# Top-k attention and a SwiGLU FFN on one core: when the first units' attention ends, and when FFN pieces may run

## Chip, core and metric

The kernel runs on one core of one Trainium2 chip. The metric is device time in microseconds (us): the median of three runs. The core has TensorE (PE in the profile, with PEld for its weight loads), VectorE (DVE), ScalarE (ACT), GpSimd (POOL) and SyncE (SP). Each has an instruction queue of its own and executes it in program order; semaphores hold an instruction back until what it reads is there.

## The reference

Attention over 8 batches of 8 heads, 576 tokens and head size 64, in which each query keeps its 32 largest scores; the output is laid out as 4608 tokens of 512 features and goes through a SwiGLU FFN with 1536 hidden features. All is fp32.

```python
scores = scale * np.matmul(q, k.transpose(0, 1, 3, 2))
kth = np.partition(scores, -top_k, axis=-1)[..., -top_k:-top_k + 1]
scores = np.where(scores >= kth, scores, -1000000000.0)
scores = scores - np.max(scores, axis=-1, keepdims=True)
attn = np.exp(scores)
attn = attn / (np.sum(attn, axis=-1, keepdims=True) + 1e-09)
attn_out = np.matmul(attn, v)
x = attn_out.transpose(0, 2, 1, 3).reshape(B * S, H * D)
g = x @ w_gate
silu = g * (1.0 / (1.0 + np.exp(-g)))
out = (silu * (x @ w_val)) @ w_out
```

## The kernel before

**Units.** Attention is cut into 160 units, numbered in the order of the list `units` (line 213): for each of 8 batches, 5 query tiles, and for each of these 4 pairs of heads. Query tiles 0 to 3 have 128 rows and two heads side by side (two-head units); tile 4 holds the last 64 rows of both heads, one above the other, and is worked like one head (one-head units: 16 to 19, 36 to 39, and so on to 156 to 159). A unit's steps, with their lines:

- `scores`: TensorE multiplies queries and keys (L250, or L236 in one-head units), ScalarE copies the result to `sc` (L255, L241).
- `select`: on VectorE, four rounds of MAX8 (L271) with three MATCH_REPLACE8 between them (L275) for each head, then a threshold compare that writes the penalty `e` (L281). A two-head unit has 14 of the first two kinds and 2 of the last, a one-head unit half.
- `penalize`: GpSimd adds scores to `e` (L291, L293). `weigh`: ScalarE takes exponentials and row sums (L302).
- `normalize`: GpSimd adds epsilon to the row sums (L312), VectorE takes reciprocals (L314), ScalarE scales `e` (L317). These are three steps of a generator that the main loop advances.
- `turn`: TensorE transposes `e` (L329), ScalarE copies it to `et` (L330).
- `values`, called by `finish_unit`: TensorE multiplies `et` and v (L349, L358), ScalarE copies the result into `xT` (L373), the transposed FFN input.

`prep` (L197, L205 on TensorE, L200, L201, L210 on ScalarE) transposes a pair's keys and queries, two units ahead of their first use.

**FFN.** It goes in 18 blocks of 256 tokens. A block can begin when `values` has written its 256 tokens for all four head pairs: block 0 after unit 7, block 1 after unit 15, block 2 after unit 27. `feed` cuts a block into 36 pieces: 24 pieces for gate and value products (L412, four matmuls each; the profile records each matmul as two), in six rounds of two gate pieces and two value pieces, and then 12 output pieces (L449, two matmuls each). After two product pieces the result is evacuated: for a gate by three ScalarE instructions (L430 to L432) and a product on GpSimd (L433), for a value by a ScalarE copy (L437) and a product on GpSimd (L438). These evacuations are not issued at once: they wait in the lists `on_act` and `on_pool` until the main loop or the next piece calls `flush`. An output tile of 128 tokens is copied by ScalarE (L460) and stored by SyncE (L389).

**Weights.** The three weight matrices are loaded in 72 chunks (L96, SyncE, 256 KB each, six buffers) and rounded to fewer bits before use. A rounding has two ScalarE instructions (L101, L106), a clamp on GpSimd (L103), a shift on VectorE (L110), an add on GpSimd (L113) and a combination on VectorE (L116). `weights` runs a small pipeline over the chunks: one step loads chunk n, does the ScalarE work and clamp of chunk n-2, the shift and add of chunk n-3 and the combination of chunk n-5. The gate and value chunks come first, the 24 chunks of `w_out` last. The loop advances it by one step for every 2.2 top-k instructions in most of `select` (in `dve`); `need`, called ahead of an FFN piece, advances it as far as that piece's weights require, all at once.

**The main loop.** The order on each engine is written out by hand: a NoSync dependency chains each engine's instructions in the order in which the loop issues them. Iteration n works on several units at once: top-k of unit n, scores of unit n+1, penalty and exponentials of unit n-1, scaling of unit n-2 (`over.pop(n - 2)`), transposes of unit n-3 (`TURN`), products with v of unit n-4 (`VALUES`). There are 164 iterations; the last four only drain. FFN pieces run where the loop calls `pieces`: up to 2, 1, 1 and 6 at four places. `credit` rations them: an iteration adds 4.6 (two heads) or 2.3 (one head), up to 8, and a piece costs 1; the drain adds none. Pieces that are left run after the loop.

Of the kernel before, what the change touches and what calls it, by code (L numbers as in the profile page):

```python
# [27 lines left out]
def kernel(  # L28
# [33 lines left out]
    NHP = H // 2  # L62
# [80 lines left out]
    def rounding(n):  # L143
        for _ in range(n):
            next(weight, None)
# [28 lines left out]
    def load_v(i):  # L174
        b, hp = pairs[i]
        h = slice(2 * hp, 2 * hp + 2)
        vt = slabs.tile([P, 2, J, D], FP32, tag="v", name="v")
        v_last = slabs.tile([R, 2, D], FP32, tag="vl", name="v_last")
        vl = vlast[i % NV]
        nc.sync.dma_start(  # L180
            vt[:].rearrange("p h j d -> p h (j d)"),
            v[b, h, 0:JP].rearrange("h (p j) d -> p h (j d)", j=J),
        )
        nc.sync.dma_start(v_last[:], v[b, h, JP:S].rearrange("h p d -> p h d"))
        for hh in range(2):
            o = hh * R
            nc.sync.dma_start(vl[o : o + R, o : o + R], v[b, 2 * hp + hh, JP:S])
        vs[i] = (vt, v_last, vl)
# [27 lines left out]
    def n_heads(qt):  # L216

        return 1 if qt == J else 2
# [39 lines left out]
    def select(n):  # L258

        nh = n_heads(units[n][1])  # L260
        sc = state[n]["sc"]
        m = small.tile([P, 2, TOP_K], FP32, tag="m", name="m", bufs=2)
        heads = [slice(t * S, (t + 1) * S) for t in range(nh)]
        rest = work.tile([P, 2 * S], FP32, tag="rest", name="rest", bufs=1)
        e = work.tile([P, 2 * S], FP32, tag="e", name="e", bufs=4)
        state[n] |= dict(m=m, e=e, heads=heads)
        cur = sc
        rounds = TOP_K // 8
        for r in range(rounds):
            for t, hs in enumerate(heads):  # L270
                nc.vector.max(m[:, t, 8 * r : 8 * r + 8], cur[:, hs])  # L271
                yield
            if r < rounds - 1:
                for t, hs in enumerate(heads):
                    nc.vector.match_replace(  # L275
                        rest[:, hs], m[:, t, 8 * r : 8 * r + 8], cur[:, hs], LOWEST
                    )
                    yield
                cur = rest
        for t, hs in enumerate(heads):  # L280
            nc.vector.tensor_scalar(  # L281
                e[:, hs], sc[:, hs], m[:, t, TOP_K - 1 : TOP_K], FAR, ALU.is_lt, ALU.mult
            )
# [24 lines left out]
    def normalize(n):  # L308
        st = state[n]
        tot, e, heads = st.pop("tot"), st["e"], st.pop("heads")  # L310
        nh = len(heads)
        nc.gpsimd.tensor_scalar_add(tot[:, 0:nh], tot[:, 0:nh], EPS)  # L312
        yield
        nc.vector.reciprocal(tot[:, 0:nh], tot[:, 0:nh])  # L314
        yield
        for t, hs in enumerate(heads):
            nc.scalar.mul(e[:, hs], e[:, hs], tot[:, t : t + 1])  # L317

    def turn(n):

        last = units[n][1] == J
        e = state[n].pop("e")
        et = work.tile([P, 2 * J + 1, P], FP32, tag="et", name="et")
        for c0, cn in ((0, J), (J, 1)) if last else ((0, J), (J, 1), (J + 1, J)):
            ps = ps_t.tile([P, 512], FP32, tag="t", name="etps")
            kl = R if last and c0 == J else P
            for c in range(cn):
                k0 = (c0 + c) * P
                nc.tensor.transpose(ps[0:kl, c * P : (c + 1) * P], e[:, k0 : k0 + kl], ident[:])  # L329
            nc.scalar.copy(  # L330
                et[0:kl, c0 : c0 + cn, :],
                ps[0:kl, 0 : cn * P].rearrange("p (c j) -> p c j", c=cn),
            )
            if c0 == J:
                yield
        state[n]["et"] = et
# [3 lines left out]
    def values(n):  # L340

        b, qt, hp = units[n]
        vt, v_last, vl = vs[b * NHP + hp]
        et = state.pop(n)["et"]
        last = qt == J
        ql = R if last else P
        av = ps_t.tile([P, P], FP32, tag="t", name="av")
        if not last:
            nc.tensor.matmul(av[:], vl[:], et[:, J, :], start=True, stop=False)  # L349
        for c in range(J + 1 if last else J):  # L350
            kl = R if c == J else P
            for hh in range(2):
                moving = (
                    et[0:kl, c, hh * R : (hh + 1) * R]
                    if last
                    else et[:, c + hh * (J + 1), :]
                )
                nc.tensor.matmul(  # L358
                    av[hh * R : (hh + 1) * R, 0:ql],
                    v_last[:, hh, :] if c == J else vt[:, hh, c, :],  # L360
                    moving,
                    start=last and c == 0,
                    stop=c == (J if last else J - 1),
                )
        c0 = b * S + qt * P
        at = c0
        while at < c0 + ql:
            kb = at // BLK
            n_c = min((kb + 1) * BLK, c0 + ql) - at
            if kb not in xT:  # L370
                xT[kb] = ffn.tile([P, NHP, BLK], FP32, tag="xT", name="xT", bufs=3)
                done[kb] = 0
            nc.scalar.copy(  # L373
                xT[kb][:, hp, at - kb * BLK : at - kb * BLK + n_c],
                av[:, at - c0 : at - c0 + n_c],
            )
            done[kb] += n_c
            at += n_c
# [88 lines left out]
    NU = len(units)  # L467
# [3 lines left out]
    def piece():  # L471

        if len(on_act) > 1:
            flush(on_act)
        if len(on_pool) > 1:
            flush(on_pool)
        while True:
            if not current:
                if not todo or done.get(todo[0], 0) < NHP * BLK:
                    return False  # L480
                flush(on_act)
                flush(on_pool)
                current.append(feed(todo.pop(0)))
            if next(current[0], 0) == 0:
                current.pop()
                continue
            return True

    def fetch(n):

        b, qt, hp = units[n]
        i = b * NHP + hp
        if qt == 0:
            yield from prep(i)
        if qt == J and i + NHP < len(pairs):
            load(i + NHP)

    def pieces(n):
        for _ in range(n):
            if credit[0] >= 1 and piece():  # L500
                credit[0] -= 1

    def run(steps):
        for _ in steps:
            pass

    def finish_unit(n):
        values(n)
        b, qt, hp = units[n]
        if qt == J and b + 1 < B:  # L510
            load_v((b + 1) * NHP + hp)
# [7 lines left out]
    credit = [0.0]  # L519
    no = iter(())  # L520
    over = {}
    TURN, VALUES = 3, 4
    due = [0.0]
    for n in range(NU + VALUES):
        nh = n_heads(units[n][1]) if n < NU else 1
        topk = select(n) if n < NU else no
        over[n - 1] = normalize(n - 1) if 0 <= n - 1 < NU else no
        nxt = scores(n + 1) if n + 1 < NU else no
        ahead = fetch(n + 2) if n + 2 < NU else no
        norm = over.pop(n - 2, no)  # L530

        def dve(k, beside=True):

            for _ in range(k * nh):
                next(topk, None)
                due[0] += 5 / 11 if beside else 0
                if due[0] >= 1:
                    due[0] -= 1
                    rounding(1)

        if n < NU:
            credit[0] = min(credit[0] + (4.6 if nh == 2 else 2.3), 8.0)
        flush(on_act)
        next(norm, None)
        if 0 <= n - 1 < NU:
            penalize(n - 1)
        flush(on_pool)
        if 0 <= n - TURN < NU:
            run(turn(n - TURN))
        if n >= VALUES:  # L550
            finish_unit(n - VALUES)
        next(nxt, None)
        if 0 <= n - 1 < NU:
            weigh(n - 1)
        run(nxt)

        dve(2, beside=False)
        if 2 <= n + 2 < NHP:
            load(n + 2)
        if n < NHP:  # L560
            load_v(n)
        pieces(2)
        flush(on_act)
        flush(on_pool)
        dve(2)
        next(norm, None)
        run(norm)
        next(ahead, None)
        pieces(1)
        next(ahead, None)  # L570
        dve(1)
        pieces(1)
        dve(2)
        run(topk)
        pieces(6)
    while piece():
# [49 lines left out]
```

## Time and profile before

| what | value |
|---|---|
| runs | 1925.72, 1926.95, 1926.94 us; median 1926.94 |
| the profiled execution's own time | 1924.16 us |
| its span, first to last instruction | 1922.4 us |
| mean granted TensorE clock | 0.958 |
| PE busy | 1759.7 us (92%) |
| DVE busy | 1608.6 us (84%) |
| ACT busy | 1156.6 us (60%) |
| POOL busy | 815.5 us (42%) |
| chain that ended last | PE 82%, DVE 6%, POOL 5%, ACT 5% |

By stretches of the trace (a unit is ended by its last L281):

| stretch, us | what runs | PE busy | DVE busy | clock |
|---|---|---|---|---|
| 0 to 138 | units 0 to 8, no FFN | 52.4 | 120.5 | 0.68 |
| 138 to 183 | units 9 to 11; FFN from 167.1 | 30.3 | 40.5 | 0.76 |
| 183 to 253 | units 12 to 15 | 56.6 | 58.2 | 0.90 |
| 253 to 292 | units 16 to 20 | 35.8 | 35.0 | 1.00 |
| 292 to 403.5 | units 21 to 30 | 103.4 | 106.4 | 0.95 |
| 403.5 to 1776 | units 31 to 156 | 1348.9 | 1229.4 | 1.00 |
| 1776 to 1821 | units 157 to 159 and the drain | 35.4 | 18.7 | 0.90 |
| 1821 to 1922.4 | FFN pieces left | 97.0 | 0 | 0.97 |

A line of the timeline reads: start in us, length in us, engine, line of the kernel, operation, tile written <- tiles read, shapes, count of instructions merged, and in brackets the engine's idle time before it and what ended that. In the slices of the page each digit is the busy share of one fortieth of the span (48 us), in tenths, and PEclk the clock granted to TensorE.

### The profile page before, as it was taken

To read this page: it belongs to the slowest core of one execution; us is meant where nothing else is said; L and a number is where in the kernel's file an instruction comes from. 1 tells how busy PE (TensorE), PEld (TensorE's weight loads), DVE (VectorE), ACT (ScalarE), POOL (GpSimd) and SP (SyncE) were. 2 spreads that over 40 slices of the span, in tenths; PEclk is the share of its full clock that TensorE was granted. 3 is DMA by queue.
4 is the path that set the end of the run, shared out by engine and by line. 5 is a ranking of instruction groups with operands and counts; after the bars stand their busy time and mean duration, and the time that the engine had idled before them with its cause. 6 is when DMAs were issued, how large, how long until landed. Compare 5 with 4: busy or idle time off the path is not lost.

```text
span 1922.4 us, 29365 instructions
## 1 busy us (share of the span) xinstructions
PE 1759.7 (92%) x10144; PEld 1299.6 (68%) x10144; DVE 1608.6 (84%) x3476; ACT 1156.6 (60%) x2821; POOL 815.5 (42%) x846
## 2 busy tenths in 40 slices
PE   3437789989999999999999999999999999999899
PEld 2326558677777777676767776767676767686666
DVE  7999889998899979997899979998899979997300
ACT  5666666566666666665666666666666656665411
POOL 4556634434354434343434343435253525353222
PEclk7668899989999999999999999999999999999899
DMA  7222212000300011000210002000200011000000
GB/s 186 88 80 77 66 27 63 11 2 2 81 7 12 7 35 49 12 6 8 58 30 1 12 16 73 1 12 2 67 22 12 1 27 38 12 1 12 1 11 11
DMA packets 111253, 59.58 MB, mean 31 GB/s; under 512 B 89088, under 2 KB 97280, under 8 KB 111104
## 3 DMA queue, kind: packets, MB, share of 16 engines
q1 hardware_dynamic: 109904, 57.41, 11.3%
q8 instruction: 80, 1.31, 0.3%
q14 instruction: 69, 0.57, 0.1%
q10 hardware_dynamic: 1200, 0.30, 0.1%
HBM read 48.23 MB, written 9.44 MB: 30 GB/s over the span
## 4 chain that ended last, share of the span: by engine, by line
PE 82%; DVE 6%; POOL 5%; ACT 5%; issue 2%; DMA 0%; SPq 0%; POOLq 0%; DVEq 0%; ACTq 0%
PE f L412 38%; PE o_ps L449 19%; PE av L358 7%; PE etps L329 7%; PE s L250 6%; DVE m L271 3%; POOL e L293 2%; DVE rest L275 2%; PE s L236 2%; PE av L349 1%; ACT e L302 1%; PE kqps L205 1%; ACT sc L255 1%; POOL size L113 1%; POOL size L103 1%
## 5 line engine op out<-in xcount | busy, mean ns | idle before, releaser
L271 DVE MAX8 m<-rest 128x8 f32<-128x576 f32 x864 | 615.3, 747 | 2.2
L275 DVE MATCH_REPLACE8 rest<-m,rest 128x576 f32<-128x576 f32 x576 | 424.2, 743 | 0.0
L412 PE MATMUL f<-xT,wg 128*128 128x256 f32 x1728 | 407.5, 386 | 0.0
L293 POOL TENSOR_TENSOR e<-e,sc 128x1152 f32<-128x1152 f32 (+1 forms) x160 | 382.6, 2391 | 44.4 <-DVE e L281 38.4
L412 PE MATMUL f<-xT,wv 128*128 128x256 f32 x1728 | 397.3, 382 | 0.0
L449 PE MATMUL o_ps<-wo,h 128*128 128x512 f32 x864 | 387.2, 598 | 0.0
L412 PEld LDWEIGHTS f<-xT,wg 128*128 128x128 f32 x1728 | 323.9, 191 | 71.7 <-issue 30.4
L412 PEld LDWEIGHTS f<-xT,wv 128*128 128x128 f32 x1728 | 326.3, 191 | 54.4 <-issue 11.3
L433 POOL TENSOR_TENSOR h<-h,half_g 128x512 f32<-128x512 f32 x108 | 138.4, 1281 | 473.3 <-ACT h L432 455.3
L329 PE MATMUL etps<-ident,e 128*128 128x128 f32 (+1 forms) x1312 | 188.4, 288 | 130.9 <-POOL size L103 46.3
L271 DVE MAX8 m<-sc 128x8 f32<-128x576 f32 x288 | 205.6, 751 | 120.7 <-ACT sc L255 77.9
L449 PEld LDWEIGHTS o_ps<-wo,h 128*128 128x128 f32 x864 | 159.6, 190 | 192.9 <-issue 186.8
L329 PEld LDWEIGHTS etps<-ident,e 128*128 128x128 f32 (+1 forms) x1312 | 159.1, 147 | 181.6 <-issue 54.7
L330 ACT COPY et<-etps 128x512 f32<-128x512 f32 (+1 forms) x448 | 184.9, 481 | 147.4 <-PE etps L329 145.8
L302 ACT ACTIVATE e<-e,bias 128x576 f32<-128x576 f32 x288 | 222.0, 776 | 73.9 <-POOL e L293 73.5
L317 ACT ACTIVATE e<-e,tot 128x576 f32<-128x576 f32 x288 | 210.4, 780 | 5.4 <-DVE tot L314 5.1
L275 DVE MATCH_REPLACE8 rest<-m,sc 128x576 f32<-128x576 f32 x288 | 211.9, 742 | 0.0
L438 POOL TENSOR_TENSOR h<-h,val 128x512 f32<-128x512 f32 x108 | 139.6, 1292 | 161.3 <-ACT val L437 161.3
L250 PE MATMUL s<-kqT 64*128 64x288 f32 x1024 | 174.4, 449 | 10.2 <-ACT kqT L210 6.4
L358 PE MATMUL av<-et,v 128*64 128x128 f32 (+1 forms) x2560 | 175.2, 283 | 0.0
L255 ACT COPY sc<-s 128x288 f32<-128x288 f32 x512 | 165.0, 410 | 2.5 <-PE s L250 2.5
L312 POOL TENSOR_SCALAR tot<-tot 128x2 f32<-128x2 f32 (+1 forms) x160 | 37.0, 231 | 305.2 <-ACT e L302 296.5
(44 smaller groups left out, 1436.5 us busy)
## 6 DMA issues: line engine op xcount, KB each, us to landing
kq_in<-in_k_dram SPq DMA_DIRECT2D x64, 128.0 KB, 2.8
v<-in_v_dram SPq DMA_DIRECT2D x32, 256.0 KB, 3.0
kq_in<-in_q_dram SPq DMA_DIRECT2D x62, 128.0 KB, 2.9
w<-in_moe_w_gate_dram SPq DMA_DIRECT2D x24, 256.0 KB, 2.7
w<-in_moe_w_val_dram SPq DMA_DIRECT2D x24, 256.0 KB, 2.7
w<-in_moe_w_out_dram SPq DMA_DIRECT2D x24, 256.0 KB, 2.5
out_dram<-o SPq DMA_DIRECT2D x40, 128.0 KB, 2.4
out_dram<-o SPq DMA_DIRECT2D x16, 256.0 KB, 2.3
```

The lines of the kernel that those rows point to most:

```text
L250: nc.tensor.matmul(ps[:, 0:half], slab[d, q0 : q0 + P], slab[d, k0 : k0 + half])
L255: nc.scalar.copy(sc[:, i * half : (i + 1) * half], ps[:, 0:half])
L271: nc.vector.max(m[:, t, 8 * r : 8 * r + 8], cur[:, hs])
L275: nc.vector.match_replace(rest[:, hs], m[:, t, 8 * r : 8 * r + 8], cur[:, hs], LOWEST)
L293: nc.gpsimd.tensor_tensor(e[:, every], e[:, every], sc[:, every], ALU.add)
L302: nc.scalar.activation(e[:, hs], e[:, hs], AF.Exp, bias=bias[:, t : t + 1], scale=scale, accum_out=tot[:, t : t + 1],)
L317: nc.scalar.mul(e[:, hs], e[:, hs], tot[:, t : t + 1])
L329: nc.tensor.transpose(ps[0:kl, c * P : (c + 1) * P], e[:, k0 : k0 + kl], ident[:])
L330: nc.scalar.copy(et[0:kl, c0 : c0 + cn, :], ps[0:kl, 0 : cn * P].rearrange("p (c j) -> p c j", c=cn),)
L358: nc.tensor.matmul(av[hh * R : (hh + 1) * R, 0:ql], v_last[:, hh, :] if c == J else vt[:, hh, c, :], moving, start=last and c == 0, stop=c ...
L412: nc.tensor.matmul(ps[:, i, :], w[:, kc, m * P : (m + 1) * P], x[:, kc, :], start=(kc == 0), stop=(kc == KC - 1),)
L449: nc.tensor.matmul(ps[:], hs[m // 2][:, m % 2, t * P : (t + 1) * P], wo[:, m, :], start=(m == 0), stop=(m == MC - 1),)
```

## The change

Iterations below `HEAD = 17` are called the head. There, a unit's scaling, transposes and products with v are done in the next iteration, behind its top-k instructions, instead of two, three and four iterations on. Outside the head the old order stands; since the head has finished units up to 15, `turn` goes on with unit 16 in iteration 19 and `finish_unit` with unit 16 in iteration 20, as before. The credit is set to 8 in each iteration of the head, in the last four units and in the drain. Two small moves come with it: the first step of `normalize` sits between two top-k instruction groups in the head, and one more place for an FFN piece lies between `turn` and `finish_unit` there.

```diff
+    HEAD = 4 * NHP + 1
     TURN, VALUES = 3, 4
     due = [0.0]
     for n in range(NU + VALUES):
+        head = n < HEAD
         nh = n_heads(units[n][1]) if n < NU else 1
         topk = select(n) if n < NU else no
         over[n - 1] = normalize(n - 1) if 0 <= n - 1 < NU else no
         nxt = scores(n + 1) if n + 1 < NU else no
         ahead = fetch(n + 2) if n + 2 < NU else no
-        norm = over.pop(n - 2, no)
+        norm = over.pop(n - 1 if head else n - 2, no)
...
-        if n < NU:
+        if head or n >= NU - NHP:
+            credit[0] = 8.0
+        else:
             credit[0] = min(credit[0] + (4.6 if nh == 2 else 2.3), 8.0)
         flush(on_act)
-        next(norm, None)
+        if not head:
+            next(norm, None)
         if 0 <= n - 1 < NU:
             penalize(n - 1)
         flush(on_pool)
-        if 0 <= n - TURN < NU:
+        if HEAD - 1 <= n - TURN < NU:
             run(turn(n - TURN))
-        if n >= VALUES:
+        if n - VALUES >= HEAD - 1:
             finish_unit(n - VALUES)
...
         flush(on_act)
         flush(on_pool)
-        dve(2)
+        dve(1)
+        if head:
+            next(norm, None)
+        dve(1)
         next(norm, None)
         run(norm)
         next(ahead, None)
@@
         next(ahead, None)
         dve(1)
         pieces(1)
+        if head and n >= 1:
+            run(turn(n - 1))
         dve(2)
+        if head and n >= 1:
+            pieces(1)
+            finish_unit(n - 1)
         run(topk)
         pieces(6)
```

## The prediction

> **What bounds the kernel now.** I read the slices of the page first.
>
> ```profile
> PE   3437789989999999999999999999999999999899
> ...
> DVE  7999889998899979997899979998899979997300
> ```
>
> One digit is 48 us. TensorE (PE) is full from the seventh slice on, but its first six are slack while VectorE (DVE) is full: the head waits for the top-k. The last two slices are TensorE alone. So there are two places to gain: TensorE's idle time in the head, and the end. The stretches of the trace say the same: TensorE works 52.4 us of the first 138, and 1348.9 of the 1372.5 between 403.5 and 1776. Next, one head unit, on VectorE:
>
> ```profile
> 124.50 1.41 DVE L271 MAX8 m<-sc 128x8 f32<-128x576 f32 x2
> ...
> 131.96 0.16 DVE L314 RECIPROCAL tot<-tot 128x2 f32<-128x2 f32 x1
> ...
> 138.05 1.41 DVE L271 MAX8 m<-sc 128x8 f32<-128x576 f32 x2
> ```
>
> Unit 8 takes 13.55 us, nearly without idle: 10.6 of top-k (units 21 to 23, which round nothing, take 10.6 each) and four weight roundings at 0.7 (L116 0.41 + L110 0.29). Last, the timeline of unit 11, where FFN pieces first run among the units:
>
> ```profile
> 172.97 0.62 ACT L430 ACTIVATE h<-f 128x512 f32<-128x512 f32 x1
> ...
> 174.46 0.47 ACT L101 ACTIVATE size<-w 128x256 f32<-128x256 f32 x1
> ...
> 177.16 0.29 DVE L110 TENSOR_SCALAR size<-size 128x256 int32<-128x256 int32 x1 [3.22 <-POOL size L103]
> ```
>
> ScalarE (ACT) works in program order. It reaches a rounding (L101) only after the evacuation of FFN pieces (L430), which waits for TensorE; VectorE then stands 3.22 us for that rounding. Units 11 to 15 idle 3.2, 2.9, 2.7, 3.5 and 2.8 us on VectorE this way. FFN pieces thus tie VectorE to TensorE's pace, which is the price of moving them forward.
>
> **How far the change reaches.** I counted pieces per unit in the instruction order of the changed program. Block 0 starts in unit 8 instead of 11, with 6, 8, 8, 8, 6 pieces in units 8 to 12 (before: 8, 4, 5, 4, 5 from 11 on); block 1 starts in 16. By unit 20 it has done 55 pieces against 40. But block 2 opens only at unit 31 in both: 72 pieces are done by unit 24 after and by 27 before, both then wait, and from 31 to 155 the two orders are alike. So the lead of 15 pieces is not carried: what counts is when unit 30 ends (403.5 now) and what the last units do. VectorE's idle time in units 11 to 30 is 24.1 us, so the head can win 24 at most.
>
> **The steps**, in the times of the profiled execution (1924.16 us, span 1922.4).
>
> *Units 0 to 7.* A unit's scaling (L317) follows the reciprocal 7.5 us into the next unit (131.96 - 124.50), and its transposes, copies and products follow there. No instruction is added on VectorE. ScalarE's roundings now queue behind copies (L330) that wait for the 2.15 us of cold transposes: 0 to 0.8 us per unit, which idles 0.3 to 1.0 already. I take 2 us (0 to 6).
>
> *Units 8 to 10.* A piece is 1.73 us (two start 3.45 apart). Unit 7's products end at 124.5 + 7.5 + 1.4 scaling + 2.2 transposes + 0.6 copies left + 2.6 products = 138.8. TensorE then has, ahead of unit 10's scores, 6 pieces: 10.4, and 1.7 for a cold start (8 records took 3.78 us at 1820.76 instead of 1.9, at a granted clock of 0.50). On ScalarE the exponentials of unit 8, the roundings and the scaling stand behind the evacuation of these. Then scores 1.2, 4 pieces 6.9, transposes 1.2, a piece 1.7, products 1.5: 163.4. Next round: 3 pieces, scores and 2 pieces (9.9), value copy, two roundings on POOL and the reciprocal (2.1), scaling 1.4, transposes, piece and products (4.4): 181.5 with small waits. VectorE ends unit 10 at 182.7 (now 166.7): **+16** (13 to 19).
>
> *Unit 11 and the weights.* Now the dearest step. The pieces of w_out call `need`: each output piece of the first half-block asks for four more rounded weights, and 49 of 72 are done when unit 10 ends. In the order, 11 roundings stand in unit 11 and 12 more ahead of unit 12's first MAX8; before, they went one per 2.2 top-k instructions, down to unit 16. How fast can they go in a burst?
>
> ```profile
> 197.86 0.73 POOL L113 TENSOR_TENSOR size<-size,ulps 128x256 int32<-128x256 int32 x1 [0.82 <-DVE size L110]
> 198.56 0.40 POOL L103 TENSOR_SCALAR size<-size 128x256 f32<-128x256 f32 x1
> 199.85 0.72 POOL L113 TENSOR_TENSOR size<-size,ulps 128x256 int32<-128x256 int32 x1 [0.90 <-DVE size L110]
> 200.55 0.40 POOL L103 TENSOR_SCALAR size<-size 128x256 f32<-128x256 f32 x1
> ```
>
> POOL waits for VectorE's L110 and L110 for POOL's L103, so a rounding can't go faster than this ring: 1.99 us here, 1.92 one step earlier. It is at best 1.57 (L103 at 7.50 and 9.07, with no L116 between). I take 1.93, and 1.57 and 2.0 as ends. Unit 11's reciprocal comes at 181.5 + 9.9 + 2.5 = 193.9 (it stands behind POOL's last product); 22 roundings follow: 42.5. ScalarE's copies of unit 10 stand amid them and wait for TensorE twice: 2 us (0 to 6). Unit 12 starts at 238.4, now 182.99: +55.4, so this step is **+39.4** (31 to 47). The eight top-k instructions left of unit 11 hide in the ring's gaps.
>
> The Trainium skill, "SBUF — State Buffer", section "Who interferes with whom", speaks against the burst: it says a VectorE instruction with two SBUF inputs, as L116 is, contends with a GpSimd instruction that reads SBUF, and that a two-port instruction is blocked outright. The trace agrees: the L116 at 186.44 took 2.45 us, not 0.41, beside POOL's L293 of 185.98 to 188.61. By the rule L116 adds its 0.41 to each step of 1.57 (22 x 1.98 = 43.6 us), and the sum below would be +35.7; without it the burst is 22 x 1.57 = 34.5 and the sum +26.6.
>
> *Units 12 to 15* have no rounding and no FFN stall left: 4 x 10.75 = 43, now 70.0 (182.99 to 252.95): **-27**. (18 of the roundings they lose are among those paid above.)
>
> *Units 16 to 20.* Unit 15's products now end some 12.5 us into unit 16 (penalty, exponentials, reciprocal 5.6, scaling 1.4, cold transposes, copies and products 5.5). Six pieces (12.1 cold) stand ahead of unit 18's scores, and ScalarE evacuates 1.8, exponentiates 1, copies scores 0.7: unit 18 starts 28.3 into unit 16, where VectorE was free at 14.5. Then 4 pieces, scores and evacuation bring unit 19 to 35.8; 2 pieces, the preparation and the transposes bring unit 20 to 42.8; it ends at 53.5. Now: 252.95 to 292.2, 39.2. **+14.3** (10 to 17), though 19 pieces run in it instead of 14.
>
> *Units 21 to 30.* Now 111.3, of which VectorE idles 5.0 and needs 106. With 17 pieces left instead of 32 TensorE is not in the way; a few waits stay in units 23 and 25. **-1.3** (-5 to 0).
>
> *Units 31 to 155* follow the same order: 0, covered by TensorE's full slices.
>
> *The end.*
>
> ```profile
> 1776.28 3.72 PE L412 MATMUL f<-xT,wg 128*128 128x256 f32 x16
> ...
> 1808.03 1.89 PE L412 MATMUL f<-xT,wg 128*128 128x256 f32 x8
> ...
> 1820.76 3.78 PE L412 MATMUL f<-xT,wg 128*128 128x256 f32 x8
> ```
>
> From 1776.28 on, the last units run at VectorE's pace with 2 pieces each; TensorE then waits among the last transposes until 1820.76, and block 16's other pieces come after. With 8, 8, 8 and 4 pieces it works through: the 8-piece unit just before took 17.4 us (1758.92 to 1776.28). So 17.4 each for units 156 and 157, 13.9 for the pieces of 158, 2.2 of transposes and products, and 6.9 for the 4 pieces of 159 put the last one's end at 1834.1; then 10.4 of drain (11.0 now, less 0.6 since POOL is free); 2.5 of cold start; then block 17, 66.6 as now: 1913.6. **-8.8** (-4 to -9.5).
>
> **Sum:** 2 + 16 + 39.4 - 27 + 14.3 - 1.3 - 8.8 = +34.6. Profiled: 1924.2 + 34.6 = 1959. The median shown, 1926.94, lies 2.8 above the profiled execution; with it 1961.5. I say **1961**. Lowest terms together +13, highest +57: 1940 to 1984.
>
> **Rivals.** *The head start pays* (the other side, 7%): TensorE's pieces fill its idle head and VectorE loses none of the 24.1 us of waits it has now, so 1927 - 24 - 9 = 1894; at its least, a few us under 1927. For it speak the idle TensorE slices. Against it: to reach even zero, the burst step would have to cost 39.4 - 34.6 = 4.8 instead of 39.4, that is 22 roundings at 0.4 us, below VectorE's own 0.7. It would need ScalarE's queue not to hold VectorE as it does in unit 11. It decides from the point where unit 12 starts before about 200 us.
> *The losses are made good later* (5%): TensorE, 15 pieces or 26 us ahead, sets the time at unit 30. Then 43.4 - 26 - 8.8 = +9: 1936. VectorE's 106 us for units 21 to 30 speak against it.
> *The loads of w_out can't keep up* (5%): 256 KB per 1.93 us is 136 GB/s, where the first slices moved 186; six buffers and 2.5 us to landing suffice. If a step took 2.6, +15: 1976.
> *The tail turns* (in the range): the pieces hold up the last scores and the drain lies as bare as now: 0 instead of -8.8, 1970.
> *No change* (3%): the head's loss is as small as the tail's gain.
>
> My forecast has 80%. Less than 0.2%, 3.9 us, can't be told from no change in this kernel. Faster 0.07, same 0.03, slower 0.90. The range reaches a little below the sum's lowest end for the second rival: 1938 to 1984.
>
> **What would show it.** L116 of w_out packed about 1.9 us apart from some 194 us on, unit 12's first MAX8 near 238; idle time before DVE L110 and L314 released by POOL, in units 9 to 11; VectorE idle before unit 18's MAX8 released by ACT sc; no FFN record from about unit 25 to 31; unit 30's end near 445; the last MAX8 well ahead of the last piece of block 16, and block 17 alone from about 43 us later than a drain shortened by 9 would start. Wrong, if unit 12 starts before 215, or unit 30 ends before 420.

## The result, and the profile after

The changed kernel takes 1948.09 us (median of four runs, 1946.9 to 1949.93) against 1926.33 (four runs, 1922.09 to 1926.95): a ratio of 1.0119, 95% interval 1.0101 to 1.0136. It is slower by some 22 us. Its profiled execution took 1946.9 us, with a span of 1945.1. The slices of its page:

```profile
PE   4449669959999999999899999999999999999999
...
DVE  7996687999799979999699989998799979999400
```

TensorE's first, third and fourth slices are fuller than before, and VectorE's fourth, fifth and seventh are emptier: part of the head's idle time has changed engines. But TensorE's fifth, sixth and ninth slices have become emptier too. At the other end, TensorE's last slices are full and VectorE stops later.

The stretches of the two traces side by side, by unit ends, in us of the profiled executions. The column "predicted" is what the prediction gave for the step.

| stretch | before | after | predicted | measured |
|---|---|---|---|---|
| units 0 to 8 | 138.1 | 140.4 | +2 | +2.3 |
| units 9 and 10 | 28.7 | 45.0 | +16 | +16.3 |
| unit 11, to unit 12's first MAX8 | 16.2 | 46.0 | +39.4 | +29.8 |
| units 12 to 15 from there | 70.0 | 46.9 | -27 | -23.1 |
| units 16 to 20 | 39.2 | 50.7 | +14.3 | +11.5 |
| units 21 to 30 | 111.3 | 108.3 | -1.3 | -3.0 |
| units 31 to 155 | 1360.8 | 1360.7 | 0 | -0.1 |
| from there to the last instruction | 158.1 | 147.1 | -8.8 | -11.0 |

The busy times of the engines in units 9 to 20 and in units 21 to 30, first of the kernel before and then of the changed one (columns: stretch, its length, busy time and count for PE, PEld, DVE, ACT and POOL, granted clock, DMA share, GB/s):

```profile
138.10:292.20 154.10, 122.77 (x660) 89.27 (x657) 133.80 (x298) 94.68 (x238) 83.27 (x111) 0.89 0.20 61
292.20:403.50 111.30, 103.15 (x618) 76.79 (x618) 106.24 (x231) 71.88 (x177) 46.29 (x42) 0.95 0.09 24
```

```profile
140.40:329.10 188.70, 148.35 (x730) 105.06 (x729) 135.85 (x297) 100.64 (x245) 92.47 (x115) 0.87 0.17 50
329.10:437.40 108.30, 84.22 (x501) 60.59 (x501) 105.83 (x231) 65.61 (x163) 37.43 (x37) 0.87 0.09 25
```

Units 9 to 20 hold 25.6 us more TensorE work (the 15 pieces brought forward) and are 34.6 us longer, while VectorE has only 2 us more. Units 21 to 30 hold 18.9 us less TensorE work and are only 3.0 shorter, since VectorE's 106 us set their time in both. TensorE then has no FFN work to go on with: no FFN record lies between 377.0 and 439.5 us (before: between 376.6 and 405.8), because block 2 opens in iteration 31 in both. So a lead of TensorE is bought at full price here and can't be cashed.

Up to unit 8 little has changed. Unit 8 on VectorE in the changed kernel:

```profile
126.82 1.41 DVE L271 MAX8 m<-sc 128x8 f32<-128x576 f32 x2
...
134.21 0.17 DVE L314 RECIPROCAL tot<-tot 128x2 f32<-128x2 f32 x1
...
140.33 1.41 DVE L271 MAX8 m<-sc 128x8 f32<-128x576 f32 x2
```

It takes 13.51 us, with the reciprocal 7.39 us in (13.55 and 7.46 before), though this is now the reciprocal of unit 7 and no longer that of unit 6.

Where the loss is paid first: unit 9, just after block 0 has opened, in the timeline of all engines of the changed kernel.

```profile
139.34 3.72 PE L412 MATMUL f<-xT,wg 128*128 128x256 f32 x16
...
149.90 1.24 PE L250 MATMUL s<-kqT 64*128 64x288 f32 x8
...
150.98 0.63 ACT L432 ACTIVATE h<-h 128x512 f32<-128x512 f32 x1
151.07 3.72 PE L412 MATMUL f<-xT,wv 128*128 128x256 f32 x16
151.50 0.77 ACT L302 ACTIVATE e<-e,bias 128x576 f32<-128x576 f32 x1
...
153.01 1.29 ACT L255 COPY sc<-s 128x288 f32<-128x288 f32 x4
...
154.83 0.59 ACT L437 COPY val<-f 128x512 f32<-128x512 f32 x1 [0.52 <-PE f L412]
...
155.56 1.27 POOL L438 TENSOR_TENSOR h<-h,val 128x512 f32<-128x512 f32 x1 [2.60 <-ACT val L437]
...
157.59 0.40 POOL L103 TENSOR_SCALAR size<-size 128x256 f32<-128x256 f32 x1
158.02 0.29 DVE L110 TENSOR_SCALAR size<-size 128x256 int32<-128x256 int32 x1 [11.68 <-POOL size L103]
```

Read it from the bottom. VectorE stands 11.68 us at a rounding step. That step waits for GpSimd, whose queue stands at a product of the FFN (L438); this waits for ScalarE's copy (L437), which waits for eight FFN pieces on TensorE, from 139.34 to 154.8. Six of them were issued at the end of iteration 8, ahead of unit 10's scores (L250). Four queues in program order pass TensorE's delay on to VectorE.

The burst of roundings in units 11 and 12, on VectorE and GpSimd:

```profile
216.99 0.29 DVE L110 TENSOR_SCALAR size<-size 128x256 int32<-128x256 int32 x1 [0.98 <-POOL size L103]
217.19 0.42 DVE L116 SCALAR_TENSOR_TENSOR wo<-w,size 128x256 int32<-128x256 int32 x1
217.43 0.77 POOL L113 TENSOR_TENSOR size<-size,ulps 128x256 int32<-128x256 int32 x1 [0.48 <-ACT size L101]
218.17 0.40 POOL L103 TENSOR_SCALAR size<-size 128x256 f32<-128x256 f32 x1
...
218.60 0.29 DVE L110 TENSOR_SCALAR size<-size 128x256 int32<-128x256 int32 x1 [0.98 <-POOL size L103]
```

The ring of VectorE and GpSimd (L110, L113, L103 and the next L110, with L116 beside) turns in 1.61 us (216.99 to 218.60), not in the 1.93 of the prediction. Of the 19 turns from 197.59 to 229.86, 13 took 1.59 to 1.62 us and the others 1.74 to 2.31. The profile names ScalarE's L101 as what released L113 here; but L113 starts 0.15 us after the end of L110 in every one of these turns, and L110 is what it reads.

And unit 18, just after block 1 has opened:

```profile
288.88 3.72 PE L412 MATMUL f<-xT,wg 128*128 128x256 f32 x16
...
299.44 1.19 PE L236 MATMUL s<-kqT 64*64 64x288 f32 x8
...
301.80 0.70 ACT L241 COPY sc<-s 128x288 f32<-128x288 f32 x2
302.59 0.76 DVE L271 MAX8 m<-sc 128x8 f32<-128x576 f32 x1 [10.11 <-POOL h L433]
```

Like unit 9: six pieces from 288.88 stand ahead of the scores of 299.44, and VectorE loses 10.11 us. The profile names GpSimd's L433 as the releaser because that ended at 302.50 too; MAX8 reads `sc`, which ScalarE's copy finished at 302.50.

### The profile page after: what moved, and what is told of

Its sections match the earlier page's. It is cut to its first block, busy times and chain, and to the rows that moved or that the text cites. A ratio compares the mean times of both kernels' runs of the same rounds, so it can differ in the third digit from the quotient of the medians.

```text
span 1945.1 us, 29406 instructions
## 1 busy us (share of the span) xinstructions
PE 1771.0 (91%) x10144; PEld 1303.9 (67%) x10144; DVE 1609.3 (83%) x3476; ACT 1158.5 (60%) x2821; POOL 816.3 (42%) x846
## 4 chain that ended last, share of the span: by engine, by line
PE 81%; DVE 7%; ACT 4%; POOL 4%; issue 2%; DMA 0%; SPq 0%; POOLq 0%; ACTq 0%; DVEq 0%
PE f L412 38%; PE o_ps L449 18%; PE av L358 7%; PE etps L329 7%; PE s L250 6%; DVE m L271 3%; DVE rest L275 3%; PE s L236 2%; POOL e L293 2%; PE av L349 1%; POOL size L113 1%; PE kqps L205 1%; ACT e L302 1%; ACT sc L255 1%; POOL size L103 1%
## 5 line engine op out<-in xcount | busy, mean ns | idle before, releaser
L293 POOL TENSOR_TENSOR e<-e,sc 128x1152 f32<-128x1152 f32 (+1 forms) x160 | 382.6, 2391 | 77.0 <-DVE e L281 68.5
L449 PE MATMUL o_ps<-wo,h 128*128 128x512 f32 x864 | 396.3, 607 | 18.7 <-DVE wo L116 18.7
L412 PE MATMUL f<-xT,wg 128*128 128x256 f32 x1728 | 403.5, 383 | 0.0
L412 PEld LDWEIGHTS f<-xT,wv 128*128 128x128 f32 x1728 | 324.5, 190 | 55.4 <-issue 12.3
L433 POOL TENSOR_TENSOR h<-h,half_g 128x512 f32<-128x512 f32 x108 | 138.7, 1284 | 441.6 <-ACT h L432 429.7
L329 PEld LDWEIGHTS etps<-ident,e 128*128 128x128 f32 (+1 forms) x1312 | 163.4, 150 | 182.3 <-issue 95.2
L317 ACT ACTIVATE e<-e,tot 128x576 f32<-128x576 f32 x288 | 210.4, 779 | 8.6 <-DVE tot L314 8.1
L438 POOL TENSOR_TENSOR h<-h,val 128x512 f32<-128x512 f32 x108 | 139.1, 1288 | 167.6 <-ACT val L437 167.5
L250 PE MATMUL s<-kqT 64*128 64x288 f32 x1024 | 169.2, 447 | 4.9 <-ACT kqT L210 4.8
L430 ACT ACTIVATE h<-f 128x512 f32<-128x512 f32 x108 | 64.5, 598 | 173.9 <-PE f L412 172.5
```

Source lines behind the costliest of these rows:

```text
L250: nc.tensor.matmul(ps[:, 0:half], slab[d, q0 : q0 + P], slab[d, k0 : k0 + half])
L293: nc.gpsimd.tensor_tensor(e[:, every], e[:, every], sc[:, every], ALU.add)
L412: nc.tensor.matmul(ps[:, i, :], w[:, kc, m * P : (m + 1) * P], x[:, kc, :], start=(kc == 0), stop=(kc == KC - 1),)
L438: on_pool.append(lambda: nc.gpsimd.tensor_mul(h[:], h[:], val[:]))
L449: nc.tensor.matmul(ps[:], hs[m // 2][:, m % 2, t * P : (t + 1) * P], wo[:, m, :], start=(m == 0), stop=(m == MC - 1),)
```

## The experiments

Every ratio is to the kernel before, run on the same chip in the same batch, with its 95% interval; it can differ by about 0.1% from the quotient of the medians, so that differences of 2 us are not read as shown. "Piece" and "iteration" are used as above.

### The end alone and the head alone

`tail_only` has the old head and the new credit in the last four units and the drain; `head_only` has the new head and the old end.

```diff
-        if n < NU:
+        if n >= NU - NHP:
+            credit[0] = 8.0
+        else:
             credit[0] = min(credit[0] + (4.6 if nh == 2 else 2.3), 8.0)
```

> The kernel before with one part of the change: the credit is 8 in the last four units and the drain; the head is the old one. Theory (the end gains by itself, the head loses by itself): the changed kernel is 33.7 us late when unit 155 ends and 22.7 late at its end, so the end gives 11; alone it should give the same 11 us: 1926.3 - 11 = 1915, with the same order of instructions from unit 155 on, and nothing changed before. Rival (the end's gain needs the head's change, for example because TensorE came less late into the last units): less than 3 us.

> The changed kernel without its end: early attention and credit 8 in the head, the old ration in the last units. Theory: the head's loss of 33.7 us stays whole, 1926.3 + 33.7 = 1960. Rival (TensorE, which is full from unit 31 on, has work in hand and gives part of it back later): 1940 to 1950.

Measured: the end alone 1915.36 us, ratio 0.9951 (0.9937 to 0.9964), so 10.5 us gained; the head alone 1957.76 us, ratio 1.0172 (1.0158 to 1.0186), so 31.9 lost. Their sum, +21.4, is the whole change (+22). The end's gain shows in the timeline of TensorE in the changed kernel:

```profile
1810.03 3.72 PE L412 MATMUL f<-xT,wg 128*128 128x256 f32 x16
...
1844.75 14.00 PE L449 MATMUL o_ps<-wo,h 128*128 128x512 f32 x32
...
1860.47 7.13 PE L449 MATMUL o_ps<-wo,h 128*128 128x512 f32 x16
...
1877.58 4.59 PE L412 MATMUL f<-xT,wg 128*128 128x256 f32 x16
```

Block 16 runs among the last units (units 157 and 158 take 17.4 us each instead of 10.4 and 8.9), and after the drain, at 1877.58, only block 17 is left.

### Is it the burst? Roundings made sooner

One line paces the roundings: 2 steps per 3 top-k instructions instead of 5 per 11, so that all 72 are done by unit 10 and no burst is left. `after_r` makes that edit in the changed kernel, `before_r` in the one before.

```diff
-                due[0] += 5 / 11 if beside else 0
+                due[0] += 2 / 3 if beside else 0
```

> The changed kernel with the weights rounded sooner: 2/3 of a step per top-k instruction instead of 5/11, so that all 72 chunks are rounded when unit 10 ends and no burst is left in units 11 and 12 (23 roundings there in the changed kernel, none here; VectorE's work is the same in sum). Theory (the burst costs because it is paced by the ring of GpSimd and VectorE): VectorE's idle time of 17.9 us in units 11 and 12 falls to about 5, its wait in unit 9 (11.7) and 18 (11.2) stays: 1948 - 13 = 1935, between 1931 and 1940. Rival (units 11 and 12 are long because of TensorE's pieces, not of the roundings): 1945 to 1951.

> The kernel before with the same sooner rounding; nothing else. Theory (in units 11 to 15 VectorE waits for roundings that stand behind FFN evacuations on ScalarE, 15.1 us in all): without roundings there most of it goes, about 8 of it: 1918, between 1914 and 1922. Rival (VectorE waits there for TensorE's pace whatever it rounds): 1925 to 1928. If the faster rounding is itself held by GpSimd or the loads in units 0 to 10, slower than 1928.

Measured: 1948.81 us (1.0123, 1.011 to 1.0137) and 1930.58 us (1.0028, 1.0017 to 1.0039). Both theories were missed: `after_r` came out where its rival stood, and `before_r` above 1928, the last case of its expectation. In the changed kernel the burst was gone from units 11 and 12 and the time was the same. Units 0 to 8 ended at 164.5 instead of 140.4, because a rounding costs VectorE its 0.7 us and a share of the ring's waits wherever it stands; unit 15 ended at 279.7 instead of 278.4. What the sooner roundings took from the first units they gave back in units 11 to 15. The waits at the opening of the blocks stayed: VectorE idled 12.3 us in unit 9 and 11.8 in unit 18. The roundings were moved here, not removed; what this shows is that their place in a burst is not where the time goes. In `before_r`, units 11 to 15 took 10.6 to 11.1 us without idle on VectorE, but unit 10 had ended 33.5 us later (200.3), unit 15 0.6 later (253.6), and unit 20 7.6 later: the FFN, still tied to iteration 11, started 33.5 us later, and from there to unit 20 TensorE was busy for 98.1 of 99.5 us.

### Early attention, early FFN, free credit: one at a time

`early_ffn_late` has the early attention, but no FFN piece before iteration 11 and the old ration; `early_rationed` lets the FFN start in iteration 8, with the old ration; `unration_head` has the old attention and a credit of 8 in each iteration of the head. None has the new end.

```diff
# early_ffn_late, on top of the early attention
-                if not todo or done.get(todo[0], 0) < NHP * BLK:
+                if not todo or now[0] < 11 or done.get(todo[0], 0) < NHP * BLK:
# unration_head, in the kernel before
-        if n < NU:
+        if n <= 4 * NHP:
+            credit[0] = 8.0
+        elif n < NU:
```

> Early attention in the head alone: FFN pieces start in unit 11 as in the kernel before, with the old ration everywhere, so pieces and roundings per unit are those of the kernel before. Theory (what costs is FFN pieces among units, in which ScalarE's order ties VectorE to TensorE; ending a unit's attention sooner costs little): 2 us late at the end of unit 10, 2 to 8 late at the end of unit 30: 1928 to 1934. Rival (the moved scaling, transposes and products are themselves the loss): above 1940.

> Early attention in the head with the old ration: block 0 starts in unit 8, with 6, 6, 5, 4, 5, 4, 5, 1 pieces (changed kernel 6, 8, 8, 8, 6), and block 1 with 6 in unit 16; the roundings pulled together are 14 in unit 13 instead of 11 and 12 in units 11 and 12. The end is the old one, so it stands against the changed kernel without its end (1957.8). Theory: unit 9's wait of 11.7 us stays, unit 18's of 11.2 stays, the burst is half as long: 4 to 12 less, 1946 to 1954. Rival (the credit of 8 is the loss, so the ration cures it): 1930 to 1936.

> The kernel before with credit 8 in the head alone: pieces start in unit 11 as before, then 8, 8, 8, 8, 4 instead of 8, 4, 5, 4, 5; attention keeps its old place. No rounding is pulled ahead of its pace until unit 15. Theory: the units 12 to 14 go at TensorE's 17.4 us for 8 pieces, where they now take 19.8, 16.3 and 18.0, and units 16 to 18 have none: 1923 to 1932. Rival (the credit of 8 alone costs what the changed kernel loses): 1940 or more.

| kernel | us | ratio (interval) | pieces by unit 20 | TensorE busy in units 9 to 20 | these units take |
|---|---|---|---|---|---|
| before | 1924.53 | 1 | 40 | 122.8 | 154.1 |
| `early_ffn_late` | 1922.16 | 0.9986 (0.9977 to 0.9995) | 40 | 120.2 | 155.2 |
| `unration_head` | 1927.94 | 1.0013 (1.0004 to 1.0023) | 48 | 133.3 | 161.4 |
| `early_rationed` | 1944.91 | 1.0097 (1.008 to 1.0114) | 53 | 147.5 | 178.1 |
| `head_only` (the batch above) | 1957.76 | 1.0172 (1.0158 to 1.0186) | 55 | | |
| the whole change (in its own batch) | 1948.09 | 1.0119 (1.0101 to 1.0136) | 55 | 148.4 | 188.7 |

Two of the expectations were missed on the low side: `early_ffn_late` (1928 to 1934) and, by a little, `early_rationed` (1946 to 1954). The early attention costs nothing that shows. Whether it gains 2 us is not shown either: the two profiles end unit 30 level (403.7 and 403.5 us), and `tail_only`, whose order up to there is that of the kernel before, ends it at 405.9. What costs is that the FFN starts in iteration 8, which the early attention makes possible: 22.8 us between `early_ffn_late` and `early_rationed`. The free credit adds some 11 to that (`head_only` 31.9 over its kernel before, `early_rationed` 20.4), or 14 by the ratios. Alone, in the old order, the credit costs 1 to 4 us by the interval of its ratio.

In `early_rationed` unit 9 takes 26.4 us (before 14.6) and unit 18 17.8 (before 6.2): with 11.9 and 11.5, the openings of the two blocks make up 23.4 of the 24.0 us by which its units 9 to 20 are longer. Its burst, 14 roundings in unit 13 (30.0 us, before 16.3), is paid back in units 14 and 15, which take 10.6 each instead of 18.0 and 15.9.

### A remedy that failed: scores and exponentials ahead of the pieces

In `after_sc` the scores of the unit after next go ahead of the last pieces of an iteration on TensorE, and in the head the exponentials and score copies go ahead of the first evacuation on ScalarE.

```diff
-        nxt = scores(n + 1) if n + 1 < NU else no
+        nxt = sooner.pop(n + 1, None) or (scores(n + 1) if n + 1 < NU else no)
...
-        flush(on_act)
         if not head:
+            flush(on_act)
             next(norm, None)
...
         if 0 <= n - 1 < NU:
             weigh(n - 1)
+        if head:
+            flush(on_act)
...
             finish_unit(n - 1)
+            sooner[n + 2] = scores(n + 2)
+            next(sooner[n + 2])
...
```

> The changed kernel with the scores of the next unit issued on TensorE ahead of the last FFN pieces of an iteration of the head, and the exponentials and score copies on ScalarE ahead of the evacuation that opened the iteration. Same work, same pieces. Theory (VectorE waits because scores and exponentials stand behind pieces): unit 18's wait falls from 11.2 to about 6, unit 9's from 11.7 to 7 or 9 (its roundings still stand behind evacuations): 1948 - 9 = 1939, between 1934 and 1944. Rival (they don't wait for the pieces in front): 1946 to 1950.

Measured: 1959.29 us, ratio 1.0168 (1.0152 to 1.0184), some 10 us slower than the change and slower than both theory and rival expected. Unit 18 did not get shorter (19.2 us, 17.3 in the change). Its timeline of all engines in unit 9 (its lines from 224 on are one further down):

```profile
149.57 2.61 POOL L294 TENSOR_TENSOR e<-e,sc 128x1152 f32<-128x1152 f32 x1
...
152.21 0.78 ACT L303 ACTIVATE e<-e,bias 128x576 f32<-128x576 f32 x1 [4.29 <-POOL e L294]
...
154.89 0.62 ACT L431 ACTIVATE h<-f 128x512 f32<-128x512 f32 x1
...
156.60 1.28 POOL L434 TENSOR_TENSOR h<-h,half_g 128x512 f32<-128x512 f32 x1 [4.42 <-ACT h L433]
...
160.41 0.29 DVE L110 TENSOR_SCALAR size<-size 128x256 int32<-128x256 int32 x1 [15.44 <-POOL size L103]
```

The exponentials (L303) now stand ahead of the evacuation (L431), and wait 4.29 us for GpSimd's penalty (L294), as they must. The evacuation starts at 154.89 instead of 150.01, GpSimd's product at 156.60 instead of 151.69, and VectorE's rounding, which waits behind it, stands 15.44 us instead of 11.68. I had looked at the wait for scores, but another one ended last. The run has both moves at once; the scores ahead on TensorE, without the exponentials ahead on ScalarE, were not tried.

### No rounding at all

In `before_nr` and `after_nr` the four rounding instructions on VectorE and GpSimd are left out: ScalarE copies the weights' high words, so the weights are not rounded. The three weight matrices are 64-bit floats, not fp32 like q, k and v: L96 loads a low and a high word for each, and a rounding makes one fp32 of the two. Without it the weights have wrong values, so these two kernels serve for times alone. VectorE then has neither a burst nor a rounding to wait at.

```diff
-        size = conv.tile([P, n], FP32, tag="size", name="size", bufs=4)
-        nc.scalar.activation(size[:], high.bitcast(FP32), AF.Abs)
-        nc.gpsimd.tensor_scalar(size[:], size[:], HUGE, LEAST, ALU.min, ALU.max)
-        ulps = conv.tile([P, n], I32, tag="ulps", name="ulps")
-        nc.scalar.mul(ulps[:], low.bitcast(U32), 2.0**-29)
+        nc.scalar.activation(dst, high.bitcast(FP32), AF.Abs)
+        nc.scalar.copy(dst, high.bitcast(FP32))
...
```

> The kernel before, with the weights' high words copied by ScalarE as they are: VectorE's and GpSimd's four rounding instructions (L103, L110, L113, L116) of all 72 chunks are left out, so the weights are not rounded; ScalarE still issues two instructions for each chunk. VectorE then sheds 72 x 0.69 = 50 us, some 3.1 us from each unit up to 16. Unit 8 should end near 113 us (138.1 before), units 9 and 10 take 10.6 each, units 11 to 15 become TensorE's (72.8 us of TensorE work there before: some 73 to 78 us), units 16 to 20 stay near 38. Expected 1878 to 1892 us. It is the yardstick for the next run.

> The changed kernel with the same left out (weights not rounded). There is then no burst of roundings, and no rounding step on VectorE that waits for GpSimd. Theory A (the head's loss is TensorE work brought forward: by unit 20 the changed kernel has issued 55 FFN pieces against 40, and units 9 to 20 hold 148.4 us of TensorE work against 122.8, which units 21 to 30 don't give back because VectorE paces them at 10.6 us): units 9 and 10 still take 40 to 45 us together (TensorE's 41.9), unit 20 ends 17 to 33 us after that of the run before it, and with the shorter end (-11) and -3 from units 21 to 30 the time is 3 to 19 us over that run, likeliest 11. Theory B (the loss is the burst of roundings and VectorE's waits in the rounding ring): units 9 to 13 take 10.6 to 14 each, unit 20 ends within 10 us of the other's, and the time is equal to that run's or up to 14 us under it.

Measured: 1864.77 us (0.9691, 0.9676 to 0.9707) and 1896.09 us (0.9853, 0.9837 to 0.9868): 31.3 us apart. Without any rounding the change loses more, not less; so the loss needs neither a burst nor a rounding. Theory B falls; theory A has the right side, but is too small (3 to 19). The yardstick, too, came out lower than expected: units 11 to 15 took 58.6 us, not 73 to 78. The changed order without roundings, units 9 to 20 and units 9 and 10 by engines:

```profile
108.40:276.50 168.10, 146.22 (x751) 106.85 (x750) 109.21 (x232) 102.92 (x249) 55.53 (x54) 0.92 0.19 54
...
108.40:150.80 42.40, 42.31 (x238) 35.09 (x238) 21.30 (x47) 28.39 (x67) 16.12 (x14) 0.99 0.20 62
```

In units 9 and 10 TensorE is busy for 42.31 of 42.40 us; the old order without roundings takes 21.1 us for them. And on VectorE of the same kernel:

```profile
127.69 0.17 DVE L314 RECIPROCAL tot<-tot 128x2 f32<-128x2 f32 x1 [13.74 <-POOL tot L312]
...
145.70 0.17 DVE L314 RECIPROCAL tot<-tot 128x2 f32<-128x2 f32 x1 [7.36 <-POOL tot L312]
```

With no rounding to stand at, VectorE stands at the reciprocal, behind GpSimd, for 13.74, 7.36 and 7.35 us (units 9, 10, 11). The wait belongs to the pieces, not to what happens to stand in front of them. Units 9 to 20 take 168.1 us against 126.6 in `before_nr`, with 146.2 us of TensorE work against 115.2: 31.0 of work brought forward and 10.5 of idle. Theory A left out that the old order with roundings is itself slowed in units 11 to 15, just where its TensorE work lies: 86.2 us with roundings and 58.6 without, in the changed order 93.0 and 75.7. So the roundings hid part of the loss.

### What can be won

`late_tail_only` has the early attention with the late, rationed FFN, and the new end. `late_tail_spread` also keeps some pieces of block 16 for the drain.

```diff
# late_tail_spread, in place of the two lines of tail_only
+        if n >= NU - NHP:
+            credit[0] = (8.0, 8.0, 4.0, 2.0)[n - NU + NHP] if n < NU else 2.0
```

> The two parts that cost nothing, together: attention ends one iteration later in the head, FFN starts in unit 11 as before with the old ration, and the last four units and the drain are not rationed. If the parts add: before 1925, less 2.4 (attention alone) and less 10.5 (the end alone) = 1912, in 1910 to 1914. Rival: the lead of 2 us is lost in the FFN's end, and the time is that of the end alone, 1914.5 to 1917.

> As the run before it, but in the last four units the credit is set to 8, 8, 4 and 2, and to 2 in each iteration of the drain, so that pieces are left for TensorE while the last units' normalization and values go through. If the drain's idle TensorE was what was left to win: 2 to 5 us under the run before it, 1907 to 1911. Rival: TensorE is not what sets the end there, or the pieces kept back only come later: within 1 us of the run before it, or slower.

Measured, against 1922.14 us of the kernel before: 1913.25 us (0.995, 0.9936 to 0.9963) and 1910.17 us (0.993, 0.9918 to 0.9942). The first ratio is that of the end alone (0.9951), so whether the early attention adds anything to it stays open. The second is the fastest of all that round the weights, ahead of both kernels. Its TensorE during the drain:

```profile
1820.18 3.70 PE L449 MATMUL o_ps<-wo,h 128*128 128x512 f32 x8
...
1826.80 3.70 PE L449 MATMUL o_ps<-wo,h 128*128 128x512 f32 x8
...
1831.85 3.70 PE L449 MATMUL o_ps<-wo,h 128*128 128x512 f32 x8
...
1841.41 3.72 PE L412 MATMUL f<-xT,wg 128*128 128x256 f32 x16
```

Two output pieces lie between the last units' products each time, and block 17's first products take 3.72 us, where after a bare drain the same 16 took 4.59 (the changed kernel) and 6.14 (`late_tail_only`). From unit 159's last top-k to the last instruction it takes 89.7 us against 94.9 in `late_tail_only` (93.3 in the changed kernel).

## Why the prediction was right, and where it was not

- **The sign and most steps were right.** The head loses, the lead is not carried, the end gains. Units 0 to 10 (+18.6, predicted +18) and units 31 to 155 came as worked out, and in unit 9 VectorE waits at L110, behind GpSimd, as foretold.
- **Some of the closeness of units 9 and 10 is luck.** The sum has 1.7 us for a cold start of TensorE ahead of the six pieces of block 0, and again for those of block 1. None was paid: both rows of six took 10.56 us at a granted clock of 1.00 (139.34 to 149.90, 288.88 to 299.44), not 12.1. In unit 9 this was made up by a wait that the sum does not have: TensorE stood 1.83 us for the scaling (L317) ahead of the transposes of 160.07.
- **The burst's step was mis-sized.** Of the 12 us between forecast (+34.6) and measurement (+22.7 in the profiled executions), 9.6 lie in unit 11 and its burst: +29.8 for +39.4. The 22 roundings (counted by L116) from the reciprocal (196.23, forecast 193.9) to unit 12's first MAX8 (231.44) took 35.2 us, 1.60 each, instead of 42.5 plus 2. The prediction took its 1.93 from steps of the trace before, in which the ring was not at its pace: from the L110 of 197.43 to that of 199.42 VectorE worked without idle, with two top-k instructions between the roundings, so GpSimd waited for VectorE's own queue. Its other bound, 1.57, was nearer, and the sum by it, +26.6, nearer still.
- **The rule weighed there.** The Trainium skill, "SBUF — State Buffer", section "Who interferes with whom", says that a VectorE instruction with two SBUF inputs contends with a GpSimd instruction that reads SBUF, and that the one issued first keeps the other out; the prediction left out this last condition. By the rule it put a turn at 1.98 us. In the burst 16 of the 22 L116 take 0.41 to 0.43 us also where L113 runs into them (217.43), and L113 0.77 instead of 0.73; the other six L116 take 0.51 to 0.98. No whole L116 is added to a turn. The measurement decides: 1.61. Beside the long L293 the rule does show: at 190.17, with L293 running to 191.14, an L116 took 1.26 us.
- **A wait was not foreseen.** Unit 13 took 15.2 us, not 10.75: VectorE stood 4.50 us at its reciprocal (252.14), whose exponentials stood on ScalarE behind the copy of an output tile. It is more than the 3.9 by which units 12 to 15 gave back less than predicted.
- **"Now the dearest step" was the wrong reading.** The burst is a long stretch of the trace, but units 11 to 15 together are only 6.7 us longer (92.9 against 86.2); the prediction's own net for them was 39.4 - 27 = +12.4, less than its +16 for units 9 and 10. `after_r` moves the burst's roundings into the first units and gains nothing; `after_nr` has no roundings and loses more. The loss is in TensorE's pieces at the openings: units 9 and 10 (+16.3) and 16 to 20 (+11.5).
- **Units 16 to 20 and the end** came 2.8 and 2.2 us better than forecast. Unit 18's first MAX8 came 24.2 us into unit 16, not 28.3; 1.5 of this is the cold start that was not paid. The end gave 11.0.
- **The rivals.** The head start did not pay, and the losses were not made good later: units 21 to 30 gave 3.0 back, VectorE's 106 us standing in both. (The highest terms of the prediction's range add up to +58, not +57.)

Open: whether letting a block's first pieces go two by two, instead of six at an iteration's end, takes away the 11 us of each opening. It was not tried; that the six pieces are what stretches these units is read from the traces, and two runs agree with it. In `early_ffn_late` block 0 opens in iteration 11 without such a row of six. In `before_nr`, without roundings, it opens there with eight pieces spread over the iteration, and units 11 and 12 take 10.7 and 11.6 us; in `after_nr` the six in a row come in iteration 8, and units 9 and 10 take 24.4 and 18.0, though with eight pieces in iteration 9 instead of four in iteration 12.

## What to carry to other kernels

Before filling an engine's idle time with work brought forward, ask whether the lead can be spent later: where another engine sets the later pace, as here, it can't, and the filled time is paid in full. Work that goes ahead of a short, urgent step on an engine that works in program order delays every queue that depends on that step; the longest wait in the profile may stand at an instruction that only happens to be next. To learn whether a conspicuous stretch costs anything, take it away: here the burst was 35 us long, yet moving its roundings elsewhere brought nothing, and the change lost no less with all roundings left out.

## What the hardware showed besides

- VectorE and GpSimd, handing 256-column chunks back and forth in a ring of three instructions (L110, L113, L103), need 1.61 us in most turns of the burst. VectorE works 0.7 us of it, with the L116 beside the ring, and stands 0.98 us ahead of L110.
- A VectorE instruction with one SBUF input was held too: at 191.35 an L110 took 1.36 us instead of 0.28, beside GpSimd's L433 of 191.10 to 192.56. In the kernel before, the L110 of 188.81 took 1.36 us beside an L438 of 188.56 to 190.02. Both ended 0.15 us after the GpSimd instruction.
